# Attention chunk by chunk with all head groups, one pass for v, an 11-product output projection and shared Exps

## The chip, the cores and the metric

The kernel runs on one core of one Trainium2 chip. The metric is device time in microseconds (us) of one execution. Inside the core, TensorE (PE; PEld are its weight loads) multiplies into PSUM's eight banks, VectorE (DVE), ScalarE (ACT) and GpSimd (POOL) compute, and SyncE (SP) issues the DMAs.

## The reference

A pre-norm transformer block on 2048 tokens of width 448, in float32: LayerNorm, sliding-window attention (16 heads of 28, window 256), residual, LayerNorm, gated feed-forward part of inner width 1792, residual.

```python
qkv = (x @ wqkv).reshape(B, S, 3, H, Dh)             # x = layernorm(A_x); H = 16, Dh = 28
scores = einsum("bhqd,bhkd->bhqk", q, k) * Dh**-0.5   # masked to 0 <= i - j < 256
o = einsum("bhqk,bhkd->bhqd", softmax(scores), v)
h = A_x + o.reshape(B, S, D) @ wo                     # D = 448
h2 = h + (gelu(layernorm(h) @ w_gate) * (layernorm(h) @ w_up)) @ w_down
```

## The kernel before

**Precision.** TensorE's fast float32 form keeps fewer bits than float32, so most operands are split into a high part (`to_hi`, an ACT copy with rounding) and a low part (`to_lo`, what is left). A product over 448 inputs is then 11 matmuls in one PSUM bank (`TERMS`: four 128-row pieces, the last overlapping, in the combinations high x high, high x low and low x high).

**Units.** Tokens come in 16 tiles of 128 and 4 chunks of 512 (`c`). Heads come in 4 groups of 4 (`g`). A block `B` is one group on one chunk: 16 blocks.

**Attention, in two passes** (`p`), each for two head groups (8 heads) over all four chunks:

- `layer_norms`, `normalise`: LayerNorm of a tile, four 128x128 transposes on TensorE (L383), high and low parts into `xT`, which holds all 2048 tokens. The second LayerNorm goes another way (`turn`): 32x32 transposes on VectorE, out to DRAM and back by DMA.
- `values` (L535): v of a tile for one pass, 11 matmuls of 224 columns; `v_m` keeps 16 tiles. `project_tile` (L580): q or k of a head group for a chunk, 11 matmuls of 512 columns, out to DRAM, and back by `loads` into a ring of two blocks (`rq`, `rk`) with high and low parts stacked on partitions.
- `scores` (L629): for a query tile and head, up to 384 keys; VectorE adds the mask and takes the row's maximum from PSUM (L633). Two alternating banks.
- `maxima` (L650 to L660): for two query tiles, the negated maxima are turned by one matmul and copied by ScalarE (L328, `rq`) into extra rows of `rq`.
- `probs` (L701, L705): scores transposed, minus maximum; one matmul and one Exp for each head and key tile `m`. A key tile meets 1, 2, 3, 3, 2, 1 query tiles (`parts`), so 128 to 384 columns. Exp writes into a ring `pp` of 9 slots of 128 columns; GpSimd's `select` (L716) zeroes what is outside the window.
- `attend` (L735): the product with v, two calls a block (three key tiles each), four heads side by side in TensorE's columns; v has a column of ones, so the sums of the probabilities come too. The bank alternates between two.
- `drain` (L758 to L763): VectorE turns the bank by 32x32 transposes, reciprocal of the sums, GpSimd multiplies, turned back, split high and low (`ohl`).
- `output` (L779, L782): for each pass, 2 groups x 3 parts = 6 matmuls a token tile, and VectorE adds the result to the residual `hres`.

**Feed-forward part.** `feed_forward` goes over 14 slices of 128 inner columns in groups (`GROUPS = [3, 4, 4, 3]`), and for each group over the chunks; a product `n` is one slice on one chunk. `product` makes gate and up (L903, L927), Gelu, their product, its split, and the down products. From `n = 4` on, matmuls come in pairs on the two halves of the array (L903); the first two are "early" (`EARLY`): their PSUM results are copied out (L950) while attention still runs. A tiny ScalarE copy (`seen`, L909) watches a bank. `weights` load and split a slice's weights into seven places.

**Order.** Nothing runs in the order in which it is written. Each operation is an `Op` with an engine, a cost, a key and dependencies; `Lists.run` takes, for each engine, the startable operation with the smallest key and so writes one fixed list for each engine. Keys are made of block numbers (16 a block) and constants such as `LAG_P`, `EDGE`, `WIN`, `LN1`. On TensorE the list runs strictly in that order.

Of the kernel before, what the change touches and what calls it, by code (L numbers as in the profile page):

```python
# [17 lines left out]
NG = 4  # L18
# [6 lines left out]
GROUPS = [3, 4, 4, 3]  # L25
# [3 lines left out]
PPB = 9  # L29
# [4 lines left out]
LAG_T = 6  # L34
LAG_P = 15
LAG_V = 10
EDGE = 9
WIN = 14
# [5 lines left out]
SWAP = -60  # L44
SOON = 2
HOLDO = 1
HOLDV = 1
AHEAD = 7
BEHIND = 5
LN1 = (0, -20, 21, 53)  # L50
# [3 lines left out]
MOVED = 0  # L54
SPANS = {"pp", "proj", "raw", "xT", "h", "rqf", "rkf", "vm", "rec0", "rec1", "rec2"}
# [165 lines left out]
def block_kernel(ctx: ExitStack, tc, x, wqk_in, wv_in, wo_in, ffn_in, out):  # L221
# [19 lines left out]
    proj_m = pool.tile([128, 7936], F32R, name="proj")  # L241
    raw_m = pool.tile([128, 1472], F32, name="raw")
    xn = [pool.tile([128, D], F32, name="xn0")]
    v_m = pool.tile([128, NT * 8 * (DH + 1)], F32, name="v")
    mt = pool.tile([128, 768], F32, name="mt")
# [3 lines left out]
    mhl = [pool.tile([128, 96], F32R, name=f"mhl{i}") for i in range(3)]  # L249
    xn.append(pool.tile([128, D], F32, name="xn1"))  # L250
# [7 lines left out]
    mx = [pool.tile([128, 2, 4], F32, name=f"mx{i}") for i in range(2)]  # L258
    rcp = [pool.tile([128, 16], F32, name=f"rcp{i}") for i in range(2)]
    back = pool.tile([128, 40], F32, name="back")  # L260
# [6 lines left out]

    fst = ExitStack()
    lp = fst.enter_context(tc.tile_pool(name="late", bufs=1))
    pp_m = lp.tile([128, 4 * PPB * 128], F32, name="pp")  # L270
    oblk = lp.tile([128, 512], F32, name="oblk")
    oT = lp.tile([128, 512], F32, name="oT")
    wos = lp.tile([128, 2, 2, D], F32R, name="wos")
    ohl = lp.tile([128, 2, 2, 512], F32R, name="ohl")
    rec = []

    def open_rec():
        fst.close()
        p = ctx.enter_context(tc.tile_pool(name="fp", bufs=1))
        rec.extend(p.tile([128, REC], F32R, name=f"rec{i}") for i in range(2))  # L280
        rec.append(p.tile([128, S], F32R, name="xh"))
# [5 lines left out]
    v = v_m.rearrange("p (t g h d) -> p t g h d", t=NT, g=2, h=4)  # L287
    mask = mt[:, 0:384]
    ge = mt[:, 0:512]
    junk = [mt[:, 384 + 192 * i:576 + 192 * i].bitcast(BF) for i in range(2)]  # L290
    wqk = [proj_m[:, 1024 * i:1024 * i + 1024].rearrange("p (h b n) -> p h b n", h=2, b=4) for i in range(4)]
    pk = proj_m[:, 4096:6144].rearrange("p (a t) -> p a t", a=4)
    wv = proj_m[:, 6144:7936].rearrange("p (h b n) -> p h b n", h=2, b=4)
    wqk_raw = [raw_m[:, 512 * i:512 * i + 512].rearrange("p (b n) -> p b n", b=4) for i in range(2)]
    wv_raw = [m[:, 0:896].rearrange("p (b n) -> p b n", b=4) for m in (pp_m, raw_m)]
# [7 lines left out]
    def WVRAW(p, b, n=1):  # L303
        return span("raw", 224 * b, 224 * n) if p else ("wvraw", b // 2)

    def WV(h, b, n=1):
        return span("proj", 6144 + 896 * h + 224 * b, 224 * n)

    def PK(a):
        return span("proj", 4096 + 512 * a, 512)  # L310

    def WQK(i, h):
        return span("proj", 1024 * i + 512 * h, 512)
# [4 lines left out]
    def XT(t):  # L318
        return span("xT", t, 1)
# [4 lines left out]
    def V(t):  # L324
        return span("vm", 8 * (DH + 1) * t, 8 * (DH + 1))
# [46 lines left out]
    def normalise(t, key, kind):  # L372
        moved = kind == "ln2" and t >= MOVED
# [11 lines left out]
        c = slice(t * 128, (t + 1) * 128)  # L385
# [4 lines left out]
        def lo():  # L390
            p = view()
            to_lo(xT[:, 4:7, c], p[:, 0:3], xT[:, 0:3, c])
            to_lo(xT[0:64, 3, c], p[64:128, 3], xT[64:128, 3, c])
# [9 lines left out]
        if moved:  # L403
            turn(t, key)
            return
        op("pe", 0.44, 0.61, key, tr, [("xn", i2), "ident"], (), b)
        op("act", 0.49, 0.605, key, lambda: to_hi(xT[:, 0:4, c], view()), (), [XT(t)], b)
# [5 lines left out]
    def turn(t, key):  # L413
        c = slice(t * 128, (t + 1) * 128)
        d = xn_d[t]
        xb, at = (v_m[:, REC:REC + D], span("vm", REC, D)) if t > 7 and t % 2 else (xn[1], ("xn", 1))
# [5 lines left out]
        put = [("xnd", t, a) for a in range(4)]  # L422
        dma(key + 0.1, 230, lambda: nc.sync.dma_start(f(xT[:, 4:7, c]), d[0:384].rearrange("(b p) t -> p b t", p=128)),
            put, [XT(t)])
        dma(key + 0.1, 80, lambda: nc.sync.dma_start(f(xT[:, 3, c]), d[D - 128:D]), put, [("xt3", t)])

        def hi():
            to_hi(xT[:, 0:3, c], f(xT[:, 4:7, c]))
            to_hi(last_hi[64:128], f(xT[64:128, 3, c]))
            to_hi(xT[0:64, 3, c], f(xT[64:128, 3, c]))  # L430

        def lo():
            to_lo(xT[:, 4:7, c], f(xT[:, 4:7, c]), xT[:, 0:3, c])
            to_lo(xT[64:128, 3, c], f(xT[64:128, 3, c]), last_hi[64:128])

        op("act", 0.7, 0.82, key + 0.2, hi, [("xt3", t)], [XT(t), "lasthi"])
        op("dve", 0.75, 0.82, key + 0.2, lo, [XT(t), "lasthi"], [XT(t)], port=True)
# [4 lines left out]
    def start():  # L442
# [7 lines left out]
        wv_load(0, -95)  # L450
        for m in range(2):
            wqk_load(m, -90 + m)
        for m in range(2):
            wqk_split(m)
        for t in range(4, 6):
            load(t, -88 + t)
        for m in range(2, 4):
            wqk_load(m, -82 + m)
            wqk_split(m)
        for t in range(6, NT):  # L460
            load(t, -80 + t)
# [17 lines left out]
        for i in range(3):  # L479
# [6 lines left out]
        op("pool", 0.9, 0.95, -10, lambda: nc.gpsimd.memset(v[:, :, :, :, DH:DH + 1], 1.0), (), ["ones"])  # L486
        wv_split(0)
# [29 lines left out]
    def wv_load(p, key):  # L517
        for i in range(2):
            dma(key, 224, lambda i=i: nc.sync.dma_start(wv_raw[p][:, 2 * i:2 * i + 2], wv_in[p][:, 2 * i:2 * i + 2]),
                (), [WVRAW(p, 2 * i, 2)], after=[got[HOLDV]] if p else ())  # L520

    def wv_split(p):
        key = 66 if p else -38
        for b in range(0, 4, 2):
            op("act", 0.47, 0.57, key, lambda b=b: to_hi(wv[:, 0, b:b + 2], wv_raw[p][:, b:b + 2]),
               [WVRAW(p, b, 2)], [WV(0, b, 2)])
            op("dve", 0.54, 0.63, key + 1, lambda b=b: to_lo(wv[:, 1, b:b + 2], wv_raw[p][:, b:b + 2], wv[:, 0, b:b + 2]),
               [WVRAW(p, b, 2), WV(0, b, 2)], [WV(1, b, 2)], port=True)

    def values(p, t):  # L530
        key = 128 * p + 8 * t - ((37 if t < 4 else 24) if not p else 12)
        b = Bank("v")
        for a in range(NP):
            h, wb, xb = TERMS[a]
            op("pe", mm(224), 0.29, key + a / 16, lambda a=a, h=h, wb=wb, xb=xb: nc.tensor.matmul(  # L535
                bank[b.k][:, 0:224], xT[:, xb, t * 128:(t + 1) * 128], wv[:, h, wb, :], start=(a == 0),
                stop=(a == NP - 1)), [XT(t), WV(h, wb)], () if a else [V(t)], b, tag="v")
        op("act", 0.29, 0.39, key + 1, lambda: to_hi(
            v[:, t, :, :, 0:DH], bank[b.k][:, 0:224].rearrange("p (g h d) -> p g h d", g=2, h=4)), ["ones"], [V(t)], b)


    def wqk_load(m, key):
        dma(key, 256, lambda: nc.sync.dma_start(wqk_raw[m % 2], wqk_in[m]), (), [WQKRAW(m % 2)])

    def wqk_split(m):
        i = m % 4
        key = -34 + 3 * m if m < 4 else 72 + m
        op("act", 0.53, 0.64, key, lambda: to_hi(wqk[i][:, 0], wqk_raw[m % 2]), [WQKRAW(m % 2)], [WQK(i, 0)])
        op("dve", 0.6, 0.7, key, lambda: to_lo(wqk[i][:, 1], wqk_raw[m % 2], wqk[i][:, 0]),
           [WQKRAW(m % 2), WQK(i, 0)], [WQK(i, 1)], port=True)  # L550
# [4 lines left out]
    def pk_at():  # L555
        n = pks[0]
        pks[0] += 1
        if n in PKX:
            o = 1024 * (PKX.index(n) + 1)
# [5 lines left out]
    def project(p, c):  # L565
        for m in range(4 * p, 4 + 3 * p):
            project_tile(p, c, m)

    def project_tile(p, c, m):
        g, s = divmod(m, 2)  # L570
        i = m % 4
        hl, both, tok = pk_at()
        B = 8 * p + 2 * c + g % 2
        b = Bank("proj")
        per = 1 if m == 6 else 2
        base = 16 * B - EDGE
        for a in range(NP):
            h, wb, xb = TERMS[a]
            key = -33 + 6 * m + a / 4 if B < 2 else base - WIN * (1 - (s * NP + a) / (per * NP))
            op("pe", mm(512) + 0.002, 0.403, key, lambda a=a, h=h, wb=wb, xb=xb: nc.tensor.matmul(  # L580
                bank[b.k], wqk[i][:, h, wb, :], xT[:, xb, c * 512:(c + 1) * 512], start=(a == 0),
                stop=(a == NP - 1)), [span("xT", 4 * c, 4), WQK(i, h)], (), b, tag="proj")
        key = -30 + 6 * m if B < 2 else base
# [11 lines left out]
    def block(B):  # L595
        p, r = divmod(B, 8)
        return 2 * p + r % 2, r // 2
# [3 lines left out]
    def loads(B):  # L601
# [11 lines left out]
        key = 16 * B - (8 if B > 1 else 24)  # L613
# [7 lines left out]
    def scores(B, i, j):  # L621
# [4 lines left out]
        s = 16 * B + 4 * i + j  # L626
# [527 lines left out]
```

## Time and profile before

| | |
|---|---|
| median of 3 runs | 735.26 us (734.21 to 735.54) |
| profiled execution | 734.23 us, of which span 732.5 us |
| TensorE clock granted | 0.999 of full |
| busy, share of the span | PE 99%, PEld 83%, DVE 54%, ACT 50%, POOL 22% |
| DMA | 79.12 MB, mean 108 GB/s |

The span is from the first to the last instruction of the profiled execution. A line such as `L701 PE MATMUL bank<-rq,rk ... x352 | 96.8, 305 | 0.9 <-ACT pp L705` names the source line, the engine, the operation, the tiles written and read, the count, the busy time in us, the mean length of one in ns, and the idle time before them with what ended it. In "PEld bank L735 <- issue: 10.9, 51, 0.4" the numbers are us in total, times, and longest. A line number can be that of a helper (L328 is `to_hi`, L331 `to_lo`). A matmul on plain float32 operands (L735) is recorded twice.

### The profile page before, as it was taken

What the parts mean: (1) busy time and instruction counts of PE and PEld (TensorE: products, weight loads), DVE (VectorE), ACT (ScalarE), POOL (GpSimd) and SP (SyncE); (2) the same over time, 40 slices, a digit from 0 to 9 for tenths busy, and PEclk for the clock granted to TensorE, in tenths of its full rate; (3) what the DMA queues carried; (4) which work ended last, traced back from release to release, by engine and by line L of the source; (5) the groups of instructions that cost most, each with busy time, mean ns of one, the idle gap of its engine ahead of it and who ended that gap; (6) DMA issues with size and microseconds to landing.
All of it is one profiled execution on the core that took longest, in us unless ns stands there. A gap on an engine that the chain in (4) does not pass through costs nothing.

```text
span 732.5 us, 15381 instructions
## 1 busy us (share of the span) xinstructions
PE 723.8 (99%) x5893; PEld 604.6 (83%) x5893; DVE 395.9 (54%) x1057; ACT 365.8 (50%) x930; POOL 160.3 (22%) x253
## 2 busy tenths in 40 slices
PE   8999999999999999999999999999999999999997
PEld 7887888788888787768888888888888888888886
DVE  7977876776677788748554223144223243233223
ACT  7668776667666888876553222243222233222221
POOL 5615343343344547462000000000000000000000
PEclk9999999999999999999999999999999999999999
DMA  8888445755565777514652000012100000001012
GB/s 285 260 280 248 146 148 179 202 178 156 162 201 160 191 229 206 147 36 102 153 174 88 1 2 1 1 43 84 43 1 2 1 1 2 1 1 52 11 42 101
DMA packets 83138, 79.12 MB, mean 108 GB/s; under 512 B 34104, under 2 KB 72952, under 8 KB 83064
## 3 DMA queue, kind: packets, MB, share of 16 engines
q1 hardware_dynamic: 83064, 78.14, 35.3%
q8 instruction: 46, 0.75, 0.4%
q14 instruction: 28, 0.23, 0.1%
HBM read 48.23 MB, written 29.36 MB: 106 GB/s over the span
## 4 chain that ended last, share of the span: by engine, by line
PE 93%; ACT 2%; DVE 2%; DMA 1%; issue 1%; POOL 0%; SPq 0%; DVEq 0%; ACTq 0%; POOLq 0%
PE bank L903 52%; PE bank L580 9%; PE bank L701 6%; PE bank L629 6%; PE bank L735 6%; PE bank L535 5%; PE bank L779 5%; PE bank L927 2%; PE bank L383 1%; ACT pp L705 1%; DVE mt L633 1%; ACT xT L328 0%; DVE hres L782 0%; DMA hres<-in_x_dram 0%; PE bank L660 0%
## 5 line engine op out<-in xcount | busy, mean ns | idle before, releaser
L633 DVE CUSTOM_DVE_ANT_0 mt<-bank,mt 128x384 bf16<-128x384 f32 (+2 forms) x256 | 127.5, 524 | 38.2 <-PE bank L629 36.4
L705 ACT ACTIVATE pp<-bank 128x384 f32<-128x384 f32 (+2 forms) x352 | 121.5, 388 | 52.4 <-PE bank L701 46.5
L967 DVE TENSOR_TENSOR mt<-bank,mt 128x512 f32<-128x512 f32 x54 | 37.1, 688 | 139.5 <-ACT mt L965 139.5
L716 POOL TENSOR_SCALAR_AFFINE_SELECT pp<-pp 128x512 f32<-128x512 f32 x120 | 75.5, 642 | 124.8 <-ACT pp L705 115.0
L580 PE MATMUL bank<-xT,proj 128*128 128x512 f32 x308 | 101.2, 402 | 0.0
L701 PE MATMUL bank<-rq,rk 104*128 104x384 f32 (+2 forms) x352 | 96.8, 305 | 0.9 <-ACT pp L705 0.6
L965 ACT ACTIVATE mt<-bank 128x512 f32<-128x512 f32 x54 | 32.2, 596 | 113.5 <-PE bank L903 113.5
L629 PE MATMUL bank<-rk,rq 84*128 84x384 f32 (+2 forms) x256 | 82.7, 344 | 0.1
L903 PE MATMUL bank<-xT,rec 64*128 64x512 f32 x656 | 82.0, 388 | 0.0
L903 PE MATMUL bank<-xT,rk 64*128 64x512 f32 x656 | 82.0, 388 | 0.0
L701 PEld LDWEIGHTS bank<-rq,rk 104*128 104x128 f32 x352 | 64.7, 189 | 19.3 <-ACT pp L705 4.8
L903 PEld LDWEIGHTS bank<-xT,rec 64*128 64x128 f32 x656 | 63.0, 184 | 12.2
L903 PEld LDWEIGHTS bank<-xT,rk 64*128 64x128 f32 x656 | 63.0, 184 | 12.2
L998 DVE TENSOR_TENSOR hres<-bank,hres 128x448 f32<-128x448 f32 x64 | 35.5, 616 | 66.1 <-PE bank L903 63.9
L328 ACT ACTIVATE proj<-mt 128x512 fp32r<-128x512 f32 x54 | 34.1, 631 | 71.8 <-DVE mt L967 52.5
L903 PE MATMUL bank<-xT,proj 64*128 64x512 f32 x533 | 66.7, 388 | 0.0
L909 ACT ACTIVATE word<-bank 1x1 f32<-1x1 f32 x162 | 25.6, 158 | 79.2 <-PE bank L903 78.6
L580 PEld LDWEIGHTS bank<-xT,proj 128*128 128x128 f32 x308 | 55.9, 190 | 6.0 <-issue 0.8
L535 PE MATMUL bank<-proj,xT 128*128 128x224 f32 x352 | 60.2, 278 | 0.1
L903 PEld LDWEIGHTS bank<-xT,proj 64*128 64x128 f32 x533 | 51.1, 184 | 10.1 <-ACT word L909 0.3
L331 DVE TENSOR_TENSOR proj<-mt,proj 128x512 fp32r<-128x512 f32 x54 | 37.3, 691 | 36.8 <-ACT proj L328 28.5
L535 PEld LDWEIGHTS bank<-proj,xT 128*128 128x128 f32 x352 | 53.0, 191 | 1.8 <-DVE hres L782 0.3
(117 smaller groups left out, 1106.6 us busy)
## 6 DMA issues: line engine op xcount, KB each, us to landing
rk<-k SPq DMA_DIRECT2D x44, 336.0 KB
rq<-q SPq DMA_DIRECT2D x32, 336.0 KB
q<-proj SPq DMA_DIRECT2D x15, 448.0 KB
raw<-in_ffn_dram SPq DMA_DIRECT2D x7, 736.0 KB
v<-in_ffn_dram SPq DMA_DIRECT2D x7, 736.0 KB
k<-proj SPq DMA_DIRECT2D x11, 448.0 KB
hres<-in_x_dram SPq DMA_DIRECT2D x16, 224.0 KB
out_dram<-hres SPq DMA_DIRECT2D x16, 224.0 KB
```

Source lines behind the costliest of these rows:

```text
L331: (eng or nc.vector).tensor_sub(dst, src, f(hi))
L535: op("pe", mm(224), 0.29, key + a / 16, lambda a=a, h=h, wb=wb, xb=xb: nc.tensor.matmul(bank[b.k][:, 0:224], xT[:, xb, t * 128:(t + 1) * 1 ...
L580: op("pe", mm(512) + 0.002, 0.403, key, lambda a=a, h=h, wb=wb, xb=xb: nc.tensor.matmul(bank[b.k], wqk[i][:, h, wb, :], xT[:, xb, c * 512: ...
L629: nc.tensor.matmul(bank[b.k][:, o:384], rq[u][0:3 * DH, j, i * 128:i * 128 + 128], rk[u][0:3 * DH, j, m0 * 128:(i + 3) * 128], start=True, ...
L633: nc.vector.tensor_tensor_reduce(junk[s % 2][:, o:384], bank[b.k][:, o:384], mask[:, o:384], 1.0, -BIG, OP.add, OP.max, mx[i // 2][:, i % ...
L701: nc.tensor.matmul(bank[b.k][:, 0:n], rk[u][0:104, j, m * 128:m * 128 + 128], rq[u][0:104, j, lo * 128:(hi + 1) * 128], start=True, stop=True)
L705: nc.scalar.activation(pp[:, j, o * 128:o * 128 + n], bank[b.k][:, 0:n], AF.Exp, scale=SCALE)
L716: nc.gpsimd.affine_select(a, a, pattern=[[0, 4], [-cm, 128]], compare_op=op_, fill=0.0, base=0, channel_multiplier=cm)
L735: nc.tensor.matmul(bank[b.k][32 * j:32 * j + DH + 1, lo * 128:(hi + 1) * 128], v[:, 4 * c - 2 + m, g % 2, j, :], pp[:, j, at[m] * 128:(at[ ...
L779: op("pe", mm(D), 0.38, wk, lambda a=a, h=h, oh=oh, wh=wh, i=i, k=k: nc.tensor.matmul(bank[k.k][:, 0:D], ohl[:, h, oh, i * 128:(i + 1) * 1 ...
L903: nc.tensor.matmul(bank[bk.k][:, 0:n], w, m, start=bool(start), stop=bool(stop), tile_position=(64 * x, 0), skip_group_check=True)
L967: op("dve", 0.605, 0.702, key + 2 * NP, lambda: nc.vector.tensor_tensor(blocks(g2), src(1), blocks(g2), op=OP.mult), [*G2, *held[1]], G2, ...
```

## The change

- **One sweep over the chunks.** The two passes are gone: for each chunk all q, k and v are made, then the four head groups' blocks follow (`block(B)` is group `B % 4`, chunk `B // 4`), then one output projection. All seven q/k weight tiles stay in `x23`.
- **x by the chunk.** `xT` (all tokens) becomes `x0`, one chunk, overwritten by the next (`x0free`). For the second LayerNorm the chunks get `x0`, two parts of `x23`, and one tile that is opened when the probabilities' ring is done. The first LayerNorm of the last chunk goes by `turn` as well (`T1 = 3`).
- **v** (`values`): 448 columns in one pass; `v_m` is a ring of 8 tiles for all heads.
- **Output projection** (`SUMS`): 11 matmuls a tile for all groups. Group 0 carries high and low parts of 16 of its 28 rows in one stationary tile; its other 12 rows wait in `kept` and ride in the 4 spare rows of groups 1, 2 and 3.
- **Maxima**: one turning matmul a block; four copies by ScalarE as before.
- **Probabilities**: heads share a bank and an Exp, four at 128 columns, two at 256. The ring has 13 slots. A block's probability matmuls stand behind all of the block before.
- **Product with v**: one call a block, one bank.
- **Feed-forward**: groups of 2, 4, 4, 4; the keys and constants of the order are new.

The core of the diff:

```diff
-GROUPS = [3, 4, 4, 3]
+GROUPS = [2, 4, 4, 4]
-PPB = 9
+PPB = 13
+VR = 8
+KEPT = 16
+SPARE = 4
...
-    xT = pool.tile([128, 7, S], F32R, name="xT")
+    x0 = pool.tile([128, 7, 512], F32R, name="x0")
+    x23 = pool.tile([128, 7168], F32R, name="x23")
...
-        moved = kind == "ln2" and t >= MOVED
+        moved = kind == "ln2" or t // 4 >= T1
...
         for a in range(NP):
             h, wb, xb = TERMS[a]
-            op("pe", mm(224), 0.29, key + a / 16, lambda a=a, h=h, wb=wb, xb=xb: nc.tensor.matmul(
-                bank[b.k][:, 0:224], xT[:, xb, t * 128:(t + 1) * 128], wv[:, h, wb, :], start=(a == 0),
+            op("pe", mm(D), 0.38, key + a / 16, lambda a=a, h=h, wb=wb, xb=xb: nc.tensor.matmul(
+                bank[b.k][:, 0:D], x0[:, xb, x:x + 128], wv[:, h, wb, :], start=(a == 0),
...
     def block(B):
-        p, r = divmod(B, 8)
-        return 2 * p + r % 2, r // 2
+        return B % NG, B // NG
...
-    def maxima(B, h):
+    def maxima(B):
...
-            nc.tensor.matmul(bank[b.k][0:72, 384:512], mhl[k][:, 0:72], one_r, start=True, stop=True)
+            nc.tensor.matmul(bank[b.k][0:104, 0:128], mhl[u][:, 0:104], one_r, start=True, stop=True)
...
-    def probs(B, m, j, o):
+    def probs(B, m, js, o):
...
         def one():
-            nc.tensor.matmul(bank[b.k][:, 0:n], rk[u][0:104, j, m * 128:m * 128 + 128],
-                             rq[u][0:104, j, lo * 128:(hi + 1) * 128], start=True, stop=True)
+            for a, j in enumerate(js):
+                nc.tensor.matmul(bank[b.k][:, a * n:a * n + n], rk[u][0:104, j, m * 128:m * 128 + 128],
+                                 rq[u][0:104, j, lo * 128:(hi + 1) * 128], start=True, stop=True)
...
-            nc.scalar.activation(pp[:, j, o * 128:o * 128 + n], bank[b.k][:, 0:n], AF.Exp, scale=SCALE)
+            nc.scalar.activation(pp[:, js[0]:js[-1] + 1, o * 128:o * 128 + n],
+                                 bank[b.k][:, 0:k * n].rearrange("p (j t) -> p j t", j=k), AF.Exp, scale=SCALE)
...
+        if g == 0:
+            op("pool", *cost(256), key + 1, lambda: mul(ob[:, :, 0:KEPT], 0, KEPT), ["oblk", ("rcp", u)], ["oblk"], port=True)
+            op("act", 0.3, 0.42, key + 1.5, lambda: to_hi(tb[:, :, 0:KEPT].bitcast(F32R), ob[:, :, 0:KEPT]), ["oblk"], ["oT0"])
+            op("pool", *cost(256), key + 1.5, lambda: nc.gpsimd.tensor_tensor(
+                tb[:, :, KEPT:32], ob[:, :, 0:KEPT], tb[:, :, 0:KEPT], op=OP.subtract), ["oblk", "oT0"], ["oT"], port=True)
+            op("pool", *cost(192), key + 1.5, lambda: mul(kept, KEPT, DH), ["oblk", ("rcp", u)], ["kept"], port=True)
...
+    SUMS = [(0, 0, 0), (0, 0, 1)] + [(g + 3 * oh, g, wh) for g in range(1, NG) for oh, wh in ((0, 0), (0, 1), (1, 0))]
...
-    for p in range(2):
-        for c in range(CS):
...
+    for c in range(CS):
...
+        for m in range(WT):
+            project(c, m)
+        op("py", 0, 0, 0, lambda: None, (), [("x0free", c)], after=L.all["proj"] + L.all["v"])
+        for g in range(NG):
+            B = NG * c + g
+            loads(B)
...
+            at = slots(B)
+            ms = range(0 if c else 2, 6)
+            for m in ms:
+                k = (4, 2, 1)[parts(m)[1] - parts(m)[0]]
+                for j in range(0, 4, k):
+                    probs(B, m, range(j, j + k), at[m])
+                select(B, m, at[m])
+            attend(B, ms, at)
+            drain(B)
+        output(c)
```

More of the change, by code (lines that the diff above doesn't have):

```diff
@@ L53 @@
 PAIRED = 4
-MOVED = 0
-SPANS = {"pp", "proj", "raw", "xT", "h", "rqf", "rkf", "vm", "rec0", "rec1", "rec2"}
+BACK = 56
+PACE = 13.0
+LN1 = -23.5
+LN1X = -36.5
+T1 = 3
+LP = 0
+VK = (-18.0, -7.0, 6.5, -6.0)
+LN2 = (140.0, 210.0, 250.0, 1012.0)
+LN2X = (204.0, 226.0, 1017.0, 1058.0)
+WK = -38.0
+PS = 0.925
+SS = 1.075
+OUT = 16.0
+OSTEP = 7.5
+LSTEP = 4.5
+V0 = -29.5
+VS = 3.0
+P0 = -96.0
+P1 = 2.0
+LD = 10.0
+WOK = 57.0
+WQ = (-96, -95, -75.0, -73.0, -80, -75, -70)
+XL = (0, -62.0, -32.0, 20.0)
+SPANS = {"pp", "proj", "raw", "x0", "x23", "h", "rqf", "rkf", "vm", "ppf", "lf"}
 SLOW = 9.0
@@ L318, in XT, with X2, XC @@
     def XT(t):
-        return span("xT", t, 1)
+        return span("x0", t % 4, 1)
+    def X2(t):
+        return span("x0", t, 1) if t < 4 else ("xt2", t)
+    def XC(c):
+        return [X2(t) for t in range(4 * c, 4 * c + 4)]
     def HR(t):
@@ new lines, in drain @@
+        op(name, *cost(448), key + 1, lambda: mul(ob[:, :, 0:DH], 0, DH), ["oblk", ("rcp", u)], ["oblk"], port=True)
+        op(name, *cost(64), key + 1, lambda: eng.tensor_copy(
+            ob[:, :, DH:32], kept[:, :, SPARE * (g - 1):SPARE * g]), ["kept"], ["oblk"], port=True)
+        op("dve", 0.625, 0.71, key + 2, lambda: nc.vector.transpose(oT, oblk), ["oblk"], ["oT", "oT0"])
+        op("act", 0.52, 0.63, key + 2, lambda: to_hi(ohl[:, g], oT), ["oT"], [("ohl", g)])
+        op(name, *cost(512), key + 3, lambda: to_lo(ohl[:, g + 3], oT, ohl[:, g], eng),
+           ["oT", ("ohl", g)], [("ohl", g + 3)], port=True)
@@ L952, in product @@
         bs = [None, None] if early else bs
-        m, o = GH[n % 2]
-        at = [span("proj", o + 512 * h, 512) for h in range(2)]
+        m, o, gname, gneed = GH[n % 2]
+        at = [span(gname, o + 512 * h, 512) for h in range(2)]
         def gh(h):
@@ L1061, in block_kernel @@
+    for cc in range(CS):
+        for i in (0, 2):
+            layer_norms(range(4 * cc + i, 4 * cc + i + 2), lambda t: LN2[t // 4] + 4 * (t % 4), "ln2")
     exps.extend(L.all["exp"])
```

484 lines of the change are left out of this document (235 added, 249 removed).

## The prediction

> **What bounds the kernel now.** I read the page first: busy shares, the clock line and the chain.
>
> ```profile
> PE 723.8 (99%) x5893; PEld 604.6 (83%) x5893; DVE 395.9 (54%) x1057; ACT 365.8 (50%) x930; POOL 160.3 (22%) x253
> ...
> PEclk9999999999999999999999999999999999999999
> ...
> PE 93%; ACT 2%; DVE 2%; DMA 1%; issue 1%; POOL 0%; SPq 0%; DVEq 0%; ACTq 0%; POOLq 0%
> ```
>
> TensorE is busy in 99% of the span, at full clock in every slice, and it carries 93% of the chain that ended last. A busy matmul may still be slow, since matmuls are pipelined. So I next cut the span into stages. The columns are the stretch, its length, and the busy time of each engine (instructions in brackets).
>
> ```profile
> core 0: us, PE busy (x) PEld busy (x) DVE busy (x) ACT busy (x) POOL busy (x), PEclk, DMA share, GB/s
> 65.00:100.00 35.00, 34.95 (x255) 28.49 (x255) 30.63 (x106) 26.23 (x68) 15.64 (x21) 1.00 0.57 176
> 135.00:170.00 35.00, 35.00 (x262) 27.39 (x261) 26.11 (x87) 23.13 (x60) 13.82 (x18) 1.00 0.59 176
> 240.00:275.00 35.00, 34.71 (x264) 27.86 (x264) 28.14 (x91) 30.07 (x76) 17.30 (x25) 1.00 0.75 204
> 310.00:342.00 32.00, 31.21 (x201) 24.11 (x201) 19.80 (x42) 22.68 (x54) 14.59 (x22) 1.00 0.25 55
> 342.00:732.00 390.00, 386.29 (x3516) 330.25 (x3516) 138.07 (x232) 116.02 (x327) 3.32 (x8) 1.00 0.13 40
> ```
>
> Up to 342 us it is attention, after that the feed-forward part, which computes the same products in both kernels. In attention, VectorE works 23 to 31 us of each 35 and ScalarE 23 to 30; no other engine is full. The third view is the chain in order of time, which gives what one matmul really costs in a row of its kind: the piece's length over its count.
>
> ```profile
> by line: PE bank L903 52.1%; PE bank L580 9.2%; PE bank L701 6.4%; PE bank L629 5.7%; PE bank L735 5.5%; PE bank L535 5.2%; PE bank L779 4.9%; PE bank L927 2.3%; PE bank L383 1.1%; ACT pp L705 0.7%; DVE mt L633 0.6%; issue 0.5%; ACT xT L328
> ...
> 10.60 0.87 PE bank L383 x8
> ...
> 27.93 2.23 PE bank L535 x20
> ...
> 287.86 1.43 PE bank L735 x24
> ...
> 330.40 5.23 PE bank L927 x22
> 335.63 4.86 PE bank L779 x24
> ...
> 346.57 379.30 PE bank L903 x3462
> ```
>
> A 448-column matmul costs 4.86/24 = 0.2025 us, a 512-column one 5.23/22 = 0.238 us, a 224-column one 2.23/20 = 0.1115 us, a transpose 0.87/8 = 0.109 us, and half a product with v 1.43 us. One piece of 379.3 us holds the feed-forward part without a break. So the time is a sum over TensorE's instructions, and the change is worth what it takes from that list, less the holes it opens.
>
> **The change, part by part.** Instruction counts are those of the two programs: 5543 matmuls before, 5328 after.
>
> *Values.* Before, v was made in two passes of 352 matmuls of 224 columns; now 176 of 448. 352 x 0.1115 = 39.2 us against 176 x 0.2025 = 35.6 us: -3.6 us. [...]
>
> *Output projection.* Twelve 448-column matmuls a tile become eleven (the low parts of head group 0 ride in spare rows of the other groups): 16 fewer, 16 x 0.2025 = -3.2 us.
>
> *LayerNorm transposes.* The last chunk's four tiles go through VectorE and DRAM instead: 64 transposes become 48, 16 x 0.109 = -1.7 us. Its price lies on other engines: four more 32x32 transposes on VectorE and 24 more DMAs in SP's queue, ahead of some q and k loads of the last chunk. They hide while outputs and scores of the chunk before last.
>
> *Maxima.* One transposing matmul a block instead of two, 16 fewer. In the timeline the next matmul starts 0.06 us after it:
>
> ```profile
> 40.80 0.22 PE L660 MATMUL bank<-one,mhl 128*72 128x128 f32 x1
> 40.86 0.45 PE L580 MATMUL bank<-xT,proj 128*128 128x512 f32 x1
> ```
>
> That is -1.0 us. A block's first probabilities now wait for all sixteen maxima of its rows, not eight; what hides that is the block before, whose probabilities come in between.
>
> *One product with v a block.* Same 352 matmuls, in 16 calls instead of 32. The cost is the break at each call's ends.
>
> ```profile
> ACT pp L705 <- PE bank L701: 46.5, 91, 2.8
> ...
> PEld bank L735 <- issue: 10.9, 51, 0.4
> ...
> PEld bank L701 <- ACT pp L705: 4.8, 15, 0.7
> ...
> PEld bank L629 <- DVE mx L633: 2.8, 10, 0.4
> ```
>
> "Issue" before L735 took 10.9 us in 51 waits. Half the calls save between 0 and 5.5 us; a join inside an unbroken series still has one short start, so I take the middle, -3.0 us.
>
> *Shared Exp.* 352 Exps become 212: four heads at 128 columns, two at 256, one at 384.
>
> ```profile
> L716 POOL TENSOR_SCALAR_AFFINE_SELECT pp<-pp 128x512 f32<-128x512 f32 x120 | 75.5, 642 | 124.8 <-ACT pp L705 115.0 <-DVE rcp L761 4.2 <-issue 1.8
> ...
> L705 ACT ACTIVATE pp<-bank 128x384 f32<-128x384 f32 x128 | 56.9, 491 | 15.6 <-PE bank L701 13.4 <-POOL ohl L331 0.6 <-DMA q<-proj 0.4
> ...
> L705 ACT ACTIVATE pp<-bank 128x256 f32<-128x256 f32 x112 | 39.5, 382 | 16.6 <-PE bank L701 13.5 <-PE bank L735 1.6 <-POOL pp L716 0.6
> ...
> L705 ACT ACTIVATE pp<-bank 128x128 f32<-128x128 f32 x112 | 26.4, 277 | 20.2 <-PE bank L701 19.6
> ```
>
> The three rows rise by some 107 ns per 128 columns from about 170 ns, so 512 columns cost about 0.60 us. Four at 0.277 become one: -0.51 us x 28; two at 0.382 become one: -0.17 us x 56; together 24 us of ScalarE. But ScalarE waited 46.5 us for these matmuls, and TensorE waited 4.8 us for ScalarE. So nearly all of it falls beside the path. Between 0 and 4.8 us come back, also since fewer matmuls have to wait for a bank; I take -2.0.
>
> Sum of what goes: -3.6 - 3.2 - 1.7 - 1.0 - 3.0 - 2.0 = -14.5 us.
>
> *The start.* All seven q/k weight tiles and the full-width v weights come first. Before x, two weight tiles and v, about 0.92 + 0.52 + 0.92 = 2.4 MB must land; before it was 1.4 MB for the first values.
>
> ```profile
> GB/s 0 38 271 314 249 256 321 303 348 394 402 402 402 404 400 404 249 23 231 100 291 260 160 276 287 233 167 333 357 296 259 155 246 309 256 348 377 328 295 372
> ```
>
> ```profile
> 9.16 1.44 PE L535 MATMUL bank<-proj,xT 128*128 128x224 f32 x9
> ...
> 11.23 1.71 PE L535 MATMUL bank<-proj,xT 128*128 128x224 f32 x13
> ...
> 13.98 0.40 PE L580 MATMUL bank<-xT,proj 128*128 128x512 f32 x1
> ```
>
> Summed from its left end (one number a us), the rate passes 1.4 MB near 7 us and 2.4 MB near 10 us. Before, values began at 9.16 us, broke off, and went on at 11.23; the first projection began at 13.98. Full-width values will begin near 10 us, so the start costs 0 to 3 us. I take +0.5, as transposes and idle fills stood there anyway. Then 5 projection tiles and 26 value matmuls, 55 x 0.238 + 26 x 0.2025 = 18 us, cover the way of q and k through DRAM before the first score.
>
> *Thin stretches.* A single 512-token buffer of normalised x replaces the full one, so a chunk's projections must end before the next chunk's LayerNorm may overwrite it. Work on TensorE is less evenly spread. Per block VectorE must do this:
>
> ```profile
> L633 DVE CUSTOM_DVE_ANT_0 mt<-bank,mt 128x384 bf16<-128x384 f32 x224 | 117.2, 549 | 31.5 <-PE bank L629 29.8
> ...
> L633 DVE DVE_READ_ACCUMULATOR2_ANT mx<- 128x1 f32 x256 | 21.1, 82 | 0.0
> ...
> L782 DVE TENSOR_TENSOR hres<-bank,hres 128x448 f32<-128x448 f32 x32 | 19.8, 618 | 13.1 <-PE bank L779 11.6 <-PE bank L701 1.3
> ...
> L760 DVE STREAM_TRANSPOSE oblk<-bank 128x512 f32<-128x512 f32 x16 | 11.4, 711 | 9.5 <-PE bank L735 9.3
> L763 DVE STREAM_TRANSPOSE oT<-oblk 128x512 f32<-128x512 f32 x16 | 11.3, 705 | 1.7 <-POOL oblk L758 1.6
> ...
> L331 DVE TENSOR_TENSOR xT<-bank,xT 128x384 fp32r<-128x384 f32 x16 | 8.8, 549 | 0.2
> ```
>
> Sixteen maxima at 117.2/224 + 0.082 = 0.605 are 9.7 us, the two 32x32 transposes 1.4, small ones 0.6: 11.7 us. Between two products with v TensorE must have as much. From the line shares above a score costs 0.057 x 732.5/256 = 0.163 us and a probability 0.064 x 732.5/352 = 0.133 us. The program's order gives three poor stretches. Between blocks 3 and 4: 16 scores, 16 probabilities, 14 projections, 8 transposes and a product of some 1.9 us, 11.0 us, while VectorE has 11.7 plus four tiles of x (4 x 0.84). Between blocks 13 and 14, and 14 and 15: 24 probabilities, 16 scores, 14 outputs and 2.7 us make 11.3 us, against 11.7 plus output adds and LayerNorm pieces. If each misses 0 to 3 us, that is 0 to 8 us; VectorE can work ahead for part of it and the trace shows only 2.8 us for such waits so far. I take +2.0.
>
> *The tail.* After the last product with v, VectorE normalises and splits it:
>
> ```profile
> 330.52 0.72 DVE L760 STREAM_TRANSPOSE oblk<-bank 128x512 f32<-128x512 f32 x1 [5.81 <-PE bank L735]
> ...
> 335.26 0.65 DVE L331 TENSOR_TENSOR ohl<-oT,ohl 128x512 fp32r<-128x512 f32 x1
> ```
>
> 335.26 + 0.65 - 330.52 = 5.4 us. TensorE's list has 20 early feed-forward matmuls there, 20 x 0.238 = 4.8 us, and 12 outputs and 29 more behind. Cover gone would cost at most the 5.4 us. The feed-forward part keeps its 3504 half-array matmuls; groups of 2, 4, 4, 4 instead of 3, 4, 4, 3 ask for chunk 3's x at product 6 rather than 9, about 15 us after attention ends. I charge nothing; if its LayerNorm came late, a few us.
>
> Total: 734.23 - 14.5 + 0.5 + 2.0 = 722.2 us, against the profiled execution's own time (span 732.5, 1.7 around it). The median of the runs shown, 735.26, is 1.0 above that execution; I forecast 722.5.
>
> **The rivals.**
> *Slower: the ring empties.* The ring of probabilities has 13 slots and a block takes 12, so a block's probabilities past its first step wait until the whole product with v of the block before has read them. After the last Exp come a select (0.64), the product (2.7), a probability and its Exp (0.8): over 4 us a block in which ScalarE has no Exp. If TensorE's list has nothing for a third of that, 1.5 x 16 = 24 us are lost: 734.2 - 14.5 + 24 = 744. It decides above 0.9 us a block. Against it: some 18 us a block, of which Exps take under 9, and projections, values, scores and outputs stand between. Chance 0.08.
> *VectorE sets the pace in the thin stretches.* All 8 us are paid, and 2 at the start: 734.2 - 14.5 + 10 = 730. For it: 30.63 of 35 us in the window 65:100, where little filler stood. Chance 0.22.
> *Width costs nothing.* Cost is in proportion to columns and v saves nothing: 722.5 + 3.6 = 726. The rows (0.1115 against half of 0.2025 = 0.101) are against it. [...]
> *The holes close too.* Fewer waits and joined calls give their upper bounds, 5.5 + 4.8, and nothing is lost: 734.2 - 9.5 - 10.3 = 714. Chance 0.17.
> *No change.* The groups differ but the path is elsewhere; the 99% speaks against it. Chance 0.03: 734 to 736.
>
> **How the numbers follow.** The forecast, 718 to 727 about 722.5, has 0.46. The range leaves out the slower case, no change and the best edge of the good one: 712 to 733. Faster by over 0.2% (1.5 us, about what a measurement of this kernel tells from no change): 0.46 + 0.22 + 0.04 + 0.17 = 0.89, of which I give none to same; same 0.03, slower 0.08.
>
> **What would show it.** In the profile after, attention should end some 12 us earlier, near 330 us, and the feed-forward piece should again be near 379 us. TensorE should stay at 99%. v's group should have 176 matmuls and its pieces 0.20 us each; products with v should come in 16 pieces of about 2.7 us; ScalarE should have some 20 us less busy time in attention. Long waits of L672 for the maxima would show the VectorE rival; long waits of L747 right after L784, the ring; a first score after 45 us, a dear start. I am wrong if the feed-forward piece changes by over 2 us or attention ends after 340 us.

## The result and the profile after

The changed kernel takes 745.11 us (median of 4 runs, 744.85 to 746.07), the kernel before 735.07: ratio 1.014, 95% interval 1.0123 to 1.0158. It is 10 us slower. The forecast was 722.5 with a range of 712 to 733. The profiled execution took 746.07 us, its span is 744.4.

The page's busy line of TensorE, its clock line and the chain, and three of the weight loads' waits (us in total, times, longest):

```profile
PE 725.7 (97%) x5678; PEld 607.0 (82%) x5678; DVE 395.0 (53%) x1013; ACT 355.2 (48%) x786; POOL 160.9 (22%) x268
...
PEclk9999989999999999999999999999999999999999
...
PE 85%; DVE 7%; issue 2%; ACT 2%; DMA 2%; SPq 1%; POOL 1%; DVEq 0%; ACTq 0%
```

```profile
PEld bank L672 <- DVE mx L676: 19.6, 66, 0.9
PEld bank L784 <- issue: 15.9, 75, 0.4
PEld bank L747 <- ACT pp L751: 5.3, 16, 0.9
```

TensorE's share of the chain fell from 93% to 85%, VectorE's rose from 2% to 7%. The scores (L672) now wait 19.6 us for the maxima, where it was 2.8. And the clock line, which was full throughout, has an 8: in that slice TensorE was granted some eight tenths of its full clock.

VectorE's own total is no larger (395.0 against 395.9 us), and a maximum is no longer by its row. The groups of the maximum after and before:

```profile
L676 DVE CUSTOM_DVE_ANT_0 mt<-bank,mt 128x384 bf16<-128x384 f32 x224 | 123.6, 552 | 36.6 <-PE bank L672 16.8 <-PE bank L623 0.5
```

```profile
L633 DVE CUSTOM_DVE_ANT_0 mt<-bank,mt 128x384 bf16<-128x384 f32 x224 | 117.2, 549 | 31.5 <-PE bank L629 29.8
```

The mean is the same, 552 against 549 ns. What differs is the idle time before it: before, 29.8 of 31.5 us have a releaser, TensorE; after, 17.3 of 36.6 have one, and some 19 us have none. The timeline of VectorE shows where they lie (start, length, operation). After, and then before:

```profile
176.17 0.52 DVE L676 CUSTOM_DVE_ANT_0 mt<-bank,mt 128x384 bf16<-128x384 f32 x1
176.62 0.08 DVE L676 DVE_READ_ACCUMULATOR2_ANT mx<- 128x1 f32 x1
176.85 0.56 DVE L676 CUSTOM_DVE_ANT_0 mt<-bank,mt 128x384 bf16<-128x384 f32 x1
177.33 0.08 DVE L676 DVE_READ_ACCUMULATOR2_ANT mx<- 128x1 f32 x1
177.33 0.69 DVE L369 TENSOR_TENSOR proj<-bank,proj 128x512 fp32r<-128x512 f32 x1
177.94 0.55 DVE L676 CUSTOM_DVE_ANT_0 mt<-bank,mt 128x384 bf16<-128x384 f32 x1
```

```profile
145.36 0.56 DVE L633 CUSTOM_DVE_ANT_0 mt<-bank,mt 128x384 bf16<-128x384 f32 x1 [0.20 <-PE bank L629]
145.84 0.08 DVE L633 DVE_READ_ACCUMULATOR2_ANT mx<- 128x1 f32 x1
145.84 0.55 DVE L633 CUSTOM_DVE_ANT_0 mt<-bank,mt 128x384 bf16<-128x384 f32 x1
```

A maximum is two records here, the operation itself and the read of its accumulator, which holds the row's maximum. After, a maximum that follows a maximum starts 0.68 us behind it (176.17 to 176.85), with 0.15 us of nothing between the end of the accumulator's read and the next start. Before, it starts 0.48 us behind it, together with the read. Behind another operation there is no pause after either: the maximum at 177.94 starts before L369 has ended (177.33 + 0.69). Over all pairs of maxima of 384 columns with no other work of VectorE between them, the median step is 0.710 us after (144 pairs) and 0.483 before (129 pairs). With 256 columns it is 0.577 against 0.353, with 128 it is 0.444 against 0.222: 0.22 us each.

The cause stands in lines of the diff that the shown core leaves out, and it has nothing to do with what the change is about. The maximum also writes its 384 masked scores, which nobody reads, into a discard tile. Before there were two, in turn; after there is one:

```diff
-    junk = [mt[:, 384 + 192 * i:576 + 192 * i].bitcast(BF) for i in range(2)]
+    junk = mt[:, 384:576].bitcast(BF)
...
-            nc.vector.tensor_tensor_reduce(junk[s % 2][:, o:384], bank[b.k][:, o:384], mask[:, o:384],
+            nc.vector.tensor_tensor_reduce(junk[:, o:384], bank[b.k][:, o:384], mask[:, o:384],
```

Each maximum overwrites what the one before wrote, so it waits for its end. The wait is in the trace: at the maximum's line VectorE's queue holds 240 semaphore instructions after, and 25 before.

```profile
L676 DVEq EVENT_SEMAPHORE  x240: 21/21/21, 41.4 to 317.1; - x120
```

```profile
L633 DVEq EVENT_SEMAPHORE  x25: 21/21/21, 56.4 to 306.3; - x25
```

By the records, 226 of the 256 maxima after wait for a semaphore that VectorE itself raises; before, 9 did. The planner does not see this wait: the one tile stands neither in the operation's reads nor in its writes. (Before, the two stood in its reads alone, which orders nothing, since no operation names them as written.)

The second finding is the clock. It falls to a half in three stretches. These are windows of TensorE's busy time ahead of and in two of them, in the kernel after (the column behind POOL is PEclk):

```profile
core 0: us, PE busy (x) PEld busy (x) DVE busy (x) ACT busy (x) POOL busy (x), PEclk, DMA share, GB/s
40.00:43.70 3.70, 3.06 (x20) 2.27 (x19) 2.35 (x11) 3.08 (x6) 0.66 (x1) 1.00 0.87 289
43.70:47.10 3.40, 3.40 (x12) 3.07 (x11) 2.79 (x13) 0.54 (x1) 0.69 (x4) 0.50 0.95 338
...
101.80:105.20 3.40, 2.26 (x8) 1.15 (x7) 3.07 (x10) 2.79 (x7) 1.22 (x3) 1.00 0.61 222
105.20:108.60 3.40, 3.15 (x9) 2.73 (x9) 2.27 (x9) 2.57 (x6) 2.86 (x4) 0.50 0.00 1
108.60:112.00 3.40, 3.40 (x12) 3.11 (x12) 1.79 (x7) 1.39 (x3) 1.87 (x3) 0.50 0.34 101
...
354.30:357.70 3.40, 2.00 (x19) 1.27 (x16) 2.60 (x5) 1.21 (x4) 0.00 (x0) 1.00 0.70 129
```

Where TensorE had holes, the granted clock then fell to a half for 3.4 us or twice that, here 13.7 us in all. Not after every hole: the last row, with 2.00 of 3.40 us busy, is followed by full clock. Nothing of the kind is in the trace before. (What the clock does behind TensorE's last matmul is left out of these counts.) The busy times are to be read with care: the ends of matmuls are modelled in the profile, so the array may have had less work than they say.

### The profile page after: what moved, and what is told of

It is laid out like the page before. It is cut to its first block, busy times and chain, and to the rows that moved or that the text cites. A ratio compares the mean times of both kernels' runs of the same rounds, so it can differ in the third digit from the quotient of the medians.

```text
span 744.4 us, 14940 instructions
## 1 busy us (share of the span) xinstructions
PE 725.7 (97%) x5678; PEld 607.0 (82%) x5678; DVE 395.0 (53%) x1013; ACT 355.2 (48%) x786; POOL 160.9 (22%) x268
## 4 chain that ended last, share of the span: by engine, by line
PE 85%; DVE 7%; issue 2%; ACT 2%; DMA 2%; SPq 1%; POOL 1%; DVEq 0%; ACTq 0%
PE bank L960 51%; PE bank L623 8%; PE bank L672 7%; PE bank L747 6%; PE bank L784 4%; PE bank L584 4%; PE bank L842 3%; DVE x L369 2%; DVE mt L676 1%; DVE bnst L398 1%; PE bank L984 1%; ACT rq L366 1%; DMA rk<-k 1%; DMA rq<-q 1%; DVE rk L558 0%
## 5 line engine op out<-in xcount | busy, mean ns | idle before, releaser
L751 ACT ACTIVATE pp<-bank 128x384 f32<-128x384 f32 (+1 forms) x212 | 105.7, 531 | 24.4 <-PE bank L747 21.2
L1025 DVE TENSOR_TENSOR mt<-bank,mt 128x512 f32<-128x512 f32 x54 | 37.1, 687 | 149.0 <-ACT mt L1023 149.0
L623 PE MATMUL bank<-x,x 128*128 128x512 f32 x308 | 94.4, 401 | 0.6 <-DVE pp L369 0.5
L672 PE MATMUL bank<-rk,rq 84*128 84x384 f32 (+2 forms) x256 | 91.2, 372 | 3.6 <-DVE mx L676 3.0
L747 PE MATMUL bank<-rq,rk 104*128 104x384 f32 (+2 forms) x352 | 84.6, 310 | 2.8 <-ACT rq L366 1.4
L960 PE MATMUL bank<-x,rk 64*128 64x512 f32 x656 | 82.1, 388 | 0.0
L960 PEld LDWEIGHTS bank<-x,rk 64*128 64x128 f32 x656 | 65.1, 184 | 9.9
L747 PEld LDWEIGHTS bank<-rq,rk 104*128 104x128 f32 x352 | 61.9, 194 | 12.6 <-ACT pp L751 5.3
L672 PEld LDWEIGHTS bank<-rk,rq 84*128 84x128 f32 x256 | 48.3, 192 | 27.0 <-DVE mx L676 19.6
L960 PE MATMUL bank<-x,proj 64*128 64x512 f32 x492 | 61.7, 388 | 3.0 <-DVE mt L1025 3.0
L623 PEld LDWEIGHTS bank<-x,x 128*128 128x128 f32 x308 | 57.7, 192 | 7.6 <-DVE pp L369 1.0
L960 PEld LDWEIGHTS bank<-x,proj 64*128 64x128 f32 x492 | 49.6, 184 | 9.9 <-issue 3.3
L842 PE MATMUL bank<-oh 128*128 128x448 f32 x176 | 49.2, 372 | 0.3 <-DVE mx L676 0.3
L584 PE MATMUL bank<-proj,x 128*128 128x448 f32 x176 | 45.6, 380 | 0.3 <-DVE proj L369 0.3
L784 PE MATMUL bank<-pp,v 128*29 128x384 f32 (+2 forms) x704 | 42.1, 386 | 0.0
```

What stands on the lines that cost most here:

```text
L584: op("pe", mm(D), 0.38, key + a / 16, lambda a=a, h=h, wb=wb, xb=xb: nc.tensor.matmul(bank[b.k][:, 0:D], x0[:, xb, x:x + 128], wv[:, h, wb ...
L672: nc.tensor.matmul(bank[b.k][:, o:384], rq[u][0:3 * DH, j, i * 128:i * 128 + 128], rk[u][0:3 * DH, j, m0 * 128:(i + 3) * 128], start=True, ...
L747: nc.tensor.matmul(bank[b.k][:, a * n:a * n + n], rk[u][0:104, j, m * 128:m * 128 + 128], rq[u][0:104, j, lo * 128:(hi + 1) * 128], start= ...
L751: nc.scalar.activation(pp[:, js[0]:js[-1] + 1, o * 128:o * 128 + n], bank[b.k][:, 0:k * n].rearrange("p (j t) -> p j t", j=k), AF.Exp, sca ...
L784: nc.tensor.matmul(bank[b.k][32 * j:32 * j + DH + 1, lo * 128:(hi + 1) * 128], v[:, (4 * c - 2 + m) % VR, 4 * g + j, :], pp[:, j, at[m] * ...
L842: op("pe", mm(D), 0.38, wk, lambda a=a, o=o, g=g, wh=wh, i=i, k=k: nc.tensor.matmul(bank[k.k][:, 0:D], ohl[:, o, i * 128:(i + 1) * 128], w ...
```

## The experiments

**1. Two discard tiles again.** The two tiles put back into the kernel after (with `mt` 768 wide again to hold them), taken in turn by the head, `junk[j % 2]`; every list keeps its order.

> The kernel after, with two discard tiles for the output of the VectorE maximum again (taken in turn), as the kernel before has them; the order of the work is kept to the instruction. Theory 1 (the single discard tile): each maximum had to wait for the end of the one before it, 0.71 us from start to start where two tiles give 0.48; some 140 pairs of 384 columns that stand back to back by 0.23 us are about 32 us of VectorE time, of which 20 to 25 us reached the end in the thin stretches. Expected: maxima 0.48 us apart, the three stretches at half clock gone, 718 to 728 us, faster than the kernel before. Rival A (the order of the work in the thin stretches, with the chunk boundary after block 3 and less work kept for the last blocks): the stalls stay, 738 us or more. Rival B (the ring of values runs empty): nothing changes, 742 to 746.

Measured: 733.57 us, ratio to before 0.9985 (0.9976 to 0.9995). 11.5 us come back; maxima back to back are 0.484 us apart again (144 pairs), and the semaphore instructions at their line are gone. But the expected 718 to 728 was missed, and so was the full clock. The profile:

```profile
core 0: 732.7 us, clock 0.988
```

```profile
PE bank L960 <- DVE mt L1025: 3.1, 1, 3.1
...
PEld bank L672 <- DVE mx L676: 2.4, 6, 0.6
```

The waits of the scores are gone, 19.6 to 2.4 us. So theory 1 holds for the wait of the maxima, but the half-clock stretches did not go: there are 17.1 us of them. The worst stands at the seam, where the feed-forward part begins:

```profile
340.50:343.90 3.40, 1.43 (x14) 0.99 (x12) 3.04 (x6) 0.89 (x3) 0.00 (x0) 1.00 0.53 103
343.90:347.30 3.40, 2.32 (x12) 2.02 (x14) 2.27 (x4) 2.99 (x6) 1.14 (x1) 0.50 0.68 146
347.30:350.70 3.40, 3.40 (x20) 3.03 (x18) 2.70 (x2) 0.95 (x4) 2.79 (x3) 0.50 0.72 148
```

And the chain there (start, length, what):

```profile
338.39 4.57 DMA xn<-xn
...
343.08 0.65 DVE xn L463
343.73 0.31 DVE hres L1056
344.04 0.12 issue
344.16 0.69 DVE mt L1025
344.85 0.14 issue
344.98 5.35 PE bank L960 x23
```

A LayerNorm tile of chunk 3 waits on VectorE (L463) for a DMA that still reads its buffer; the residual adds and the gated product (L1025) are queued behind it, and TensorE waits 3.1 us for that product, then runs at half clock for 6.8 us.

**2. One discard tile in the kernel before.** `junk[s % 2]` becomes `junk[0]`, nothing else.

> The kernel before, with one discard tile in place of two; the order of the work is kept. Theory 1: maxima back to back go from 0.48 to 0.71 us; VectorE gets up to 129 x 0.23 = 30 us more to do in the attention, of which the thin stretches pass on 5 to 25: 740 to 760 us. Rivals A and B: the discard tile is not what made the kernel after slow; under 738.

Measured: 744.0 us, ratio 1.0131 (1.0116 to 1.0146). 9.2 us for one index, at full clock, with the step at 0.709 us (129 pairs) and 208 semaphore instructions at the maximum's line in place of 25. The two runs together settle it: the discard tile costs either kernel about as much as the change's whole loss.

**3. Idle matmuls in the holes.** The planner fills TensorE's early holes with transposes of the identity, up to 26 us; here to the end of attention and the seam.

```diff
-WARM = 26.0
+WARM = 400.0
```

> The kernel after with two discard tiles, and 79 idle 128-column transposes of the identity set into those places of TensorE's list where the order leaves it without work (near 40, 91 to 100, 284 to 302 and 341 us); nothing else is moved and no hole is closed, so the work still waits as before. Without them (the run with two discard tiles) the granted clock falls to a half for 17.1 us in all, right behind stretches in which TensorE is idle for a fifth or more. Theory 2 (the clock): the half-clock stretches are a consequence of the holes and cost up to 17.1/2 = 8.5 us beside the holes themselves; with the holes filled the clock stays at 1.0 and the time is 725 to 729 us. Rival (the holes alone cost): filling gives nothing, or costs up to some 2 us where a fill is in the way: 733 to 736 us.

Measured: 728.42 us, ratio 0.9904 (0.9889 to 0.992), and the clock:

```profile
core 0: 726.8 us, clock 1.000
```

That is 6.7 us below the kernel before and, by the two ratios, 0.8% or 6 us below run 1, by work that computes nothing. The same stretches now read:

```profile
337.00:340.40 3.40, 3.40 (x32) 3.04 (x31) 3.05 (x6) 0.93 (x3) 0.00 (x0) 1.00 0.51 95
340.40:343.80 3.40, 3.40 (x31) 2.90 (x31) 2.12 (x4) 3.00 (x6) 1.17 (x1) 1.00 0.73 148
```

The work still waits as before, but the clock stays full (0.999 or 1.000 in all four executions); theory 2 holds. What the holes did was less than the text of this run expected: in run 1 TensorE was busy 3.00 of 3.40 us ahead of the fall at 101.5, so idle for an eighth and not "a fifth or more". And in the kernel after, the clock fell behind a stretch that was mostly busy, 3.06 of 3.70 us ahead of the fall at 43.7. What in a hole brings the fall about was not shown.

**4. The old feed-forward groups.** Run 1 with one more line back:

```diff
-GROUPS = [2, 4, 4, 4]
+GROUPS = [3, 4, 4, 3]
```

> The kernel after with two discard tiles, and the feed-forward groups of before, 3, 4, 4, 3, in place of 2, 4, 4, 4: the early feed-forward products end later than the first group's sums are needed. Theory 3 (the seam): TensorE's 3.1 us wait for the gated product at the start of the feed-forward part, and the 6.8 us at half clock behind it, go or become short; the feed-forward part comes back from 391.8 us to 386 to 388: 727 to 730 us. Rival (the wait comes from the LayerNorm of the last chunk on VectorE, whatever the groups): the wait stays, 732 to 735 us.

Measured: 731.18 us, ratio 0.9938 (0.9914 to 0.9962), somewhat above the expected 727 to 730. The 3.1 us wait and the fall behind it are gone, and from the first half-array product to the last matmul it is 387.9 us (336.21 to 724.11) in place of 391.8. Two half-clock stretches in attention remain.

**5. Each head's Exp apart.** On run 1, in the same order.

```diff
-            nc.scalar.activation(pp[:, js[0]:js[-1] + 1, o * 128:o * 128 + n],
-                                 bank[b.k][:, 0:k * n].rearrange("p (j t) -> p j t", j=k), AF.Exp, scale=SCALE)
+            for a, j in enumerate(js):
+                nc.scalar.activation(pp[:, j, o * 128:o * 128 + n], bank[b.k][:, a * n:a * n + n], AF.Exp, scale=SCALE)
```

> The kernel after with two discard tiles, and each head's Exp apart again in the place of the shared one (352 Exps in place of 212), in the same order of everything. By the prediction's term the shared Exp is worth 0 to 4.8 us on the path, 2 taken, of about 24 us of ScalarE time: 734 to 739 us, 736 by the value taken. Rival (ScalarE is on the path of a block in this order, as a bank of probabilities now waits for one long Exp): 10 us or more, 743 us and up. Other rival (the long Exp delays the bank): faster than 733.

Measured: 736.16 us, ratio 1.0017 (1.0003 to 1.003), but its single times lie between 733.41 and 738.05, with a mean clock of 0.995 to 0.985: with the holes left open, the clock fell further in some executions than in others. So run 9 repeats it with the holes filled.

**6. Fill and groups together** (runs 1, 3 and 4).

> Two discard tiles, groups 3, 4, 4, 3, and idle transposes in the holes that remain. If theories 2 and 3 both hold, the seam's wait is gone and the clock stays at 1.0: 722 to 727 us, the fastest of these. If only the clock counts: as the run with the holes filled. If neither: 733 us.

Measured: 727.06 us, ratio 0.9887 (0.9871 to 0.9903), four times within 0.6 us, clock 1.000, at the upper edge of the expected 722 to 727. Against run 3 the old groups bring 1.4 us. This is the fastest version, 8 us faster than the kernel before and 18 faster than the change as it was made.

**7. The kernel after, one tile, with the fills.** `WARM = 400.0` alone.

> The kernel after, with its one discard tile and its groups, and the same 79 idle transposes in the planned holes. It had 13.7 us at half clock, worth up to 6.8 us. Theory 2 (the clock follows the holes) gives 738 to 742; theory 1 leaves the rest, as the maxima still wait for one another: 9 to 13 us above the run with two discard tiles and fills (728.4), so 738 to 741. Rival (one discard tile costs mainly through the clock): with the holes filled the tile costs under 4 us, 729 to 732. Rival (fills do nothing without a second tile): 743 to 746.

Measured: 742.01 us, ratio 1.0095 (1.008 to 1.011). The fills bring 3 us at one tile. At full clock the single tile costs 742.01 - 728.42 = 13.6 us, a little more than the 9 to 13 expected.

**8. A control: fills in the kernel before.**

> A control: the kernel before, with idle transposes in its planned holes (33 of them). It never fell to half clock, so theory 2 expects no gain: 734 to 737 us. If fills help by another way than the clock, it is faster by 2 us or more.

Measured: 734.4 us, ratio 0.9989 (0.9978 to 1.0001). No gain that can be told from none: the fills brought something only where the clock had fallen, some 6 us in run 3 and 3 in run 7.

**9. Exps apart, at full clock.** Run 6 with the edit of run 5.

> Two discard tiles, groups 3, 4, 4, 3, fills, and each head's Exp apart again, in the same order; the clock should stay full, so the shared Exp is measured without its chance falls. The prediction's term: 0 to 4.8 us, 2 taken, so 727 to 732, 729 by the value. Rival (ScalarE on the path): 735 or more.

Measured: 731.44 us, ratio 0.9947 (0.9932 to 0.9962); one fall of 3.4 us in its profile. Against run 6 that is 0.6% or 4.4 us. Part of it is the clock: three of its four executions had 0.998, and the one at 1.000 took 729.87 us, 2.8 above run 6. So the shared Exp is worth some 3 to 4.4 us, inside the range of 0 to 4.8 and above the 2.0 taken.

**10. The planner is told of the single tile.** On run 7, the tile in the maximum's reads and writes:

```diff
-        op("dve", 0.08 + (384 - o) * 0.00104, 0.165 + (384 - o) * 0.00106, s, most, ["mask"],
-           [("mx", B % 2, i, j)], b, tag="most")
+        op("dve", 0.08 + (384 - o) * 0.00104, 0.165 + (384 - o) * 0.00106, s, most, ["mask", "junk"],
+           [("mx", B % 2, i, j), "junk"], b, tag="most")
```

> The kernel after, with its one discard tile, its groups and idle transposes in the planned holes, but the planner is told that each maximum must wait for the one before (the tile is named in the maximum's reads and writes), so it may put other VectorE work between two maxima. The run with fills and the old order was 742.0. If the order can hide the wait, as another operation between two maxima covers it: 729 to 734. If VectorE has too little other work at the right time: 736 to 742. If the new order is worse elsewhere: above 742.

Measured: 746.13 us, ratio 1.0157 (1.0138 to 1.0177), the worst of the three outcomes named. That is 4 us above run 7 (2.9 by the spans, 743.1 and 740.2): the planner found little to put between, 126 of 224 maxima of 384 columns still follow a maximum (144 with the old order), and TensorE's idle transposes rose from 19.2 to 28.5 us. The scores do wait less for maxima, 8.9 us in place of 16.9, but the time went into other holes, and in three of the four executions the clock fell as well (0.995 and 0.996). This planner's order does not hide the wait; the second tile removes it.

## Why the prediction was wrong

For each kind of work, the time from each matmul's start to the next one's, summed over the trace (us). Waits fall to the matmul before them; "idle" are the transposes of the identity. The early feed-forward products and the last few matmuls, some 24 to 25 us in each column, are left out.

| | before | after | run 1 | run 6 |
|---|---|---|---|---|
| values | 41.5 | 39.6 | 37.2 | 37.3 |
| output projection | 40.5 | 39.2 | 38.5 | 37.9 |
| LayerNorm transposes | 6.5 | 5.9 | 5.8 | 5.5 |
| maxima | 2.5 | 1.6 | 1.4 | 1.4 |
| product with v | 43.3 | 41.4 | 41.1 | 41.0 |
| scores | 48.9 | 59.6 | 51.7 | 47.1 |
| probabilities | 53.2 | 56.0 | 54.2 | 51.3 |
| projections | 75.7 | 75.9 | 74.4 | 73.4 |
| feed-forward, half array | 384.0 | 386.7 | 389.5 | 383.8 |
| idle | 5.7 | 7.5 | 7.8 | 16.6 |

**What goes was about right.** In run 6, at full clock, values gave -4.2 us (-3.6 forecast), output -2.6 (-3.2), transposes -1.0 (-1.7), maxima -1.1 (-1.0), the product with v -2.3 (-3.0): together -11.2, where these terms forecast -12.5. The shared Exp gave 2.8 to 4.4 in place of 2.0 (run 9). "Width costs nothing", the rival with 0.04 by which v saves nothing, is not borne out by these 4.2.

The term for the product with v came out near for another reason than the one given. It was taken from the "issue" waits of its weight loads, 10.9 us, and those did not shrink with half the calls: they are 15.9 us after. What shrank is the step at each call's end: a call of 48 matmuls takes 2.73 us in the chain, where two of 24 took 1.43 each, so 0.13 us less; 16 times that is about the 2.3 measured.

**The step that failed is the price of a maximum in the thin stretches.** It read "Sixteen maxima at 117.2/224 + 0.082 = 0.605 are 9.7 us" and rested on rows of a kernel with two discard tiles. The lengths in a row overlap, so it was too dear for two tiles (0.483 us from start to start, 7.7 us a block) and too cheap for one (0.710, 11.4 us a block). With the 2 us of other work that the prediction counted, VectorE then has 13.4 us a block, where the poor stretches of TensorE's list have 11 (the first, by the prediction's own terms, 10.8). Where +2.0 stood for all such waits, the single tile alone cost 11.5 us (run 1) to 13.6 (runs 3 and 7). With two tiles the scores wait only 2.4 us for maxima (run 1). The line stood in the diff and was not priced.

**The tail was charged nothing and cost about 5 us in run 1.** The prediction did say that the new groups ask earlier for chunk 3's x, with "a few us" if it came late, and charged nothing. Run 1's chain above shows what was late: the product that TensorE needs stood behind a LayerNorm step in VectorE's queue. From the first half-array product to the last matmul it took 391.8 us there, against 386.3 before; in the kernel after 389.1 (350.98 to 740.09).

**The clock was not in the sum at all.** Every hole was charged its own length; the falls behind them, 17.1 us at half clock in run 1, are by estimate (half of that time) worth up to 8.5 us more, and run 3 got 6 of them back. From run 1 to run 6, the seam, its fall and the others together give 1.0% or 7 us by the ratios.

What then remains between run 6 (727.1) and the forecast (722.5): 1.3 us that the first five terms fell short, and waits. Idle matmuls rose by 10.9 us; some 2 of them lie in the start (+0.5 forecast; the first 26 us hold all the idle ones of run 1, 7.8 against 5.7), the rest in thin stretches later on, while scores, probabilities and projections take 6.0 us less than before.

**The rivals.** "VectorE sets the pace in the thin stretches" had the mechanism and its sign, long waits of L672 for maxima, but its 730 was worked out with the same price. "The ring empties" named 744, and 745 came; that is chance. L747 waits 5.3 us for ScalarE, hardly more than the 4.8 before, no matmul of L747 follows directly on one of L784, where the ring's waits should have stood, and runs 1 and 3 gain 11.5 and 16.7 us with the ring as it is. The slower outcome had 0.08, and none of that was for the cause that decided it.

**The signs named** read as follows: attention ended at 351 us, not 330 ("wrong if after 340"); the long feed-forward piece is 378.5 us for 3455 matmuls, as forecast, but begins late; TensorE 97%, not 99; ScalarE's Exps 105.7 us in place of 121.5, some 16 less where 20 were named; the first score came at 40.7 us, before the 45 that would have shown a dear start; products with v come in pieces of 2.73 us (2.08 on the first chunk), as forecast.

```profile
359.28 378.50 PE bank L960 x3455
```

## What to carry to other kernels

An output that nobody reads is still a buffer: with one copy of it, the maxima here took turns (0.710 us from start to start in place of 0.483), while the busy total (395.0 against 395.9 us) and the row's mean (552 against 549 ns) looked unchanged and the planner saw nothing. Compare start-to-start steps, and look in a group's idle column for time without a releaser; when a diff moves a tile from two copies to one, price the wait first. In this kernel a hole on TensorE cost more than its length where the clock fell behind it (some 6 us came back in run 3, with the holes filled), so look at the clock behind each hole, and either close holes or keep TensorE busy in them.

## What was unexpected of the hardware

The wait of one maximum for the one before it, on the same tile, cost 0.22 us each time that no other VectorE work stood between them, whatever the width (128, 256 or 384 columns). Over a kernel that is 9 to 14 us (9.2 in run 2, 11.5 by run 1, 13.6 by runs 3 and 7). Whether it is so for other operations than these maxima, each with an accumulator's read, was not shown.

That holes of 0.4 to 0.7 us by the busy rows, in 3.4 to 3.7, can come ahead of a half clock for the next 3.4 or 6.8 us was also new. It is so in some executions and not in others: of run 9's four, three had 0.998 of the clock and one 1.000. How much work keeps the clock full was not shown: windows with 1.43 to 3.06 us busy were followed by a fall, one with 2.00 in the kernel after was not, nor was 40.00 to 43.70 in run 1 with 2.94.
